# Where the routing's one-hot rows are issued between the operations of an attention tile

## The chip, the cores and the metric

One core of a Trainium2 chip. The metric is the device time of one execution in microseconds (us); lower is better. The engines of the core are named as in the profile: PE (TensorE, matrix products and transposes; PEld is its weight load), DVE (VectorE), ACT (ScalarE), POOL (GpSimd) and SP (SyncE, which here only issues DMAs). Each engine runs its own list of instructions in the order in which the kernel's text emits them; between engines, semaphores hold an instruction until its operands are there and its destination is free.

## The reference

Attention over pooled keys and values for 8 batches, 8 heads, 576 positions and a head width of 64, and then a mixture of experts with one expert for each token:

```python
k_p = k.reshape(B, H, Sp, 8, D).mean(axis=3)
v_p = v.reshape(B, H, Sp, 8, D).mean(axis=3)
scores = scale * np.matmul(q, k_p.transpose(0, 1, 3, 2))
scores = scores - np.max(scores, axis=-1, keepdims=True)
attn = np.exp(scores)
attn = attn / (np.sum(attn, axis=-1, keepdims=True) + 1e-09)
x = np.matmul(attn, v_p)                          # to 4608 tokens of 512
...
logits = x @ w_gate + modality_bias[modality_id]  # 8 experts
e_idx = np.argmax(logits, axis=1)
gate_w = softmax(logits)[np.arange(N), e_idx]
for e in range(E):
    mask = e_idx == e
    h = np.maximum(x[mask] @ w1[e], 0.0)
    out[mask] = gate_w[mask, None] * (h @ w2[e])
```

## The kernel before

**Attention.** The 4608 tokens are 36 tiles of 128. A step handles two tiles (one, in the steps that join the last 64 positions of two batches); there are 20 steps, five for each pair of batches, and a 21st pass that drains the last. The loop is software-pipelined: pass n makes the scores of its own second half and of the first half of step n + 1, and turns the probabilities of step n - 1 into output. For each half, PE writes the scores to PSUM (`s_pe`, L533), DVE takes the maximum of each row (`s_dve`, L540) and subtracts it (L543), and ACT takes the exponential (`s_act`, L555 and L556). For each tile of the step before, PE transposes the probabilities (L562, L574), ACT copies them (L567, L581), PE multiplies them with the values and with the gate's weights (`a_pe`, L597 and L601), and DVE divides (`x_dve`): the sum (L620), its reciprocal (L622), the gate's logits (L624), and the output's halves (L626, L631; for tiles of groups 2 and 3 ACT copies the second half undivided, L629). The result of `a_pe` has a single buffer in PSUM, so the products of a tile can begin when the tile before has been divided. POOL meanwhile pools keys and values by folding them in half three times (`fold`, L304 to L306).

**Routing.** The 36 tiles make four groups of nine. When a group's logits are there, `route` computes, by some 20 small DVE operations, the chosen expert (L680 to L691), the gate (L708 to L713, with the DMAs that write it beside the tokens) and the rank of each token within its expert. The counting is a set of matmuls (`pe` in `route`, L698 to L702), and what follows it (L725 to L736) splits the rank into a low part of 7 bits and a high part. Last come nine one-hot rows (L738), one for each tile: 128 x 128 in bf16, one where the column equals the token's low part. The rows are the left operand of a later product that turns ranks into lists of token numbers.

For group 0, `first_expert` (L748 to L754) follows: it finds the expert of the first token and loads it into a register of SP, so that the weights of that expert can be fetched early. For group 1, `early_table` follows: a count (`count`, a matmul on PE, L783), DVE operations (L793 to L799), the product of the rows with token numbers (`product`, L789), DVE operations that finish the indices (L763 to L767), and four gathers (L143, indirect DMAs that POOL issues) that fetch the tokens of the first two slots of 256 into `xg`. In step 17 PE transposes the first slot's gathered tokens (`x_transposes`, L161; ACT and DVE split them into two parts, L163 and L164), and from step 18 on the first matmuls of the experts (`first0`) run between the last attention steps.

**The order.** It is written out by hand. The DVE work of groups 0 to 2 stands in a list, `drip`, to which passes 6, 11 and 16 append a group's operations. Places in the loop called `gap` take up to n operations off its head: two between maximum and subtraction, one behind the sum, one behind the reciprocal, two at the end of a tile's division, and two more in the loop behind each place where a tile is divided. Functions in `held` (the matmuls of `route`, `count` and `product`) are not taken by a `gap`. They leave through `release`, at one place in each pass, just behind the scores' matmuls of the second half:

```python
            if due:
                release()
...
            run(hook_2, n)
            finish()
            due = bool(drip) and drip[0] in held
            if two:
                a_pe(old[1])
            if two:
                x_dve(old[1])
```

So `due` is set in one pass, ahead of the second tile's division, and acts in the next. Other work is bound to fixed passes by hooks: the transposes of the gathered tokens to passes N - 3 = 17 (`hook_2` and `hook_3`), and splits of the experts' weights to `hook_1` to `hook_3` (ACT L829, DVE L139).

**The experts.** Behind the attention, 18 or more slots of 256 tokens go through their expert's two matrices (PE L170 and L1155), with weights loaded by SP (L126, L129), split by ACT (L136) and DVE (L139), gathered by POOL (L143) and scattered to the output (L1141). The last group's routing is issued by hand in the first of these slots.

Of the kernel before, what the change touches and what calls it, by code (L numbers as in the profile page):

```python
# [30 lines left out]
def kernel(  # L31
# [31 lines left out]
    GROUPS = [(GT * i, GT) for i in range(B // 2)]  # L63
# [50 lines left out]
    def load_regs(s, e_ap, c_ap):  # L114
        e = nc.values_load(e_ap, engines=SP_ENGINE, min_val=0, max_val=E - 1,
                           skip_runtime_bounds_check_because="a sum over at most one expert's index")
        c = None
        if c_ap is not None:
            c = nc.values_load(c_ap, engines=SP_ENGINE, min_val=0, max_val=1,
                               skip_runtime_bounds_check_because="a comparison's result")  # L120
        regs[s] = (e, c)
# [69 lines left out]
    with ExitStack() as actx:  # L191
# [281 lines left out]
                tile_group[t] = (g, t - t0)  # L473
        drip, held, stores = [], set(), []

        def gap(n=2):

            for _ in range(n):
                if drip and drip[0] not in held:
                    drip.pop(0)()  # L480

        def release():
# [120 lines left out]
        def x_dve(t):  # L603
            n, z = tile_step[t]
            g, gi = tile_group[t]
# [24 lines left out]
            else:  # L630
                nc.vector.tensor_tensor(xo[:, 0:D // 2].rearrange("p (h d) -> p h d", h=4),  # L631
                                        avv[:, 0, :, 0:HD], rb[:, 0].to_broadcast([P, 4, HD]), op=ALU.mult)
            gap(2)

            if mixed:
                for y in range(2):
# [25 lines left out]
        def route(g):  # L662

            t0, n = GROUPS[g]
# [13 lines left out]
            ops = []  # L678
# [57 lines left out]
            add(lambda: V.tensor_copy(rh[:, sl], rki))  # L736
            for i in range(n):
                add(lambda i=i: V.tensor_scalar(arow[:, t0 + i, :], iota_b, rkf[:, i:i + 1], None, op0=ALU.is_equal))  # L738
            return ops

        def first_expert():

            V = nc.vector
            t8 = ap.tile([P, E], F32, name="t8")
            e0 = ap.tile([P, 1], F32, name="e0")
            rot = ap.tile([P, E], F32, name="rot")
            return [
                lambda: V.tensor_mul(t8, e0oh, iota_f[:, 0:E]),  # L748
                lambda: V.reduce_sum(e0, t8, axis=AX.X),
                lambda: (V.tensor_copy(meta0, e0[0:1, :]), load_regs(0, meta0[0:1, 0:1], None)),  # L750
                lambda: V.tensor_scalar(rot, iota_f[:, 0:E], e0, None, op0=ALU.subtract),
                lambda: V.tensor_scalar(t8, rot, 0.0, float(E), op0=ALU.is_lt, op1=ALU.mult),
                lambda: V.tensor_add(rot, rot, t8),
                lambda: V.tensor_tensor(lmat, rot.rearrange("p (o e) -> p o e", o=1).to_broadcast([P, E, E]),  # L754
                                        rot.rearrange("p (e o) -> p e o", o=1).to_broadcast([P, E, E]), op=ALU.is_lt),
            ]
# [53 lines left out]
        def at(hook, n, *fns):  # L810
            hook.setdefault(n, []).extend(fns)

        for n, (b, jj, _) in enumerate(steps):
            if b + 1 < B:
                if jj == 0:
                    m = n if b else n + 1
# [3 lines left out]
                if jj == 1:  # L820
                    m = n if b else n + 1
# [9 lines left out]
        for g in range(len(GROUPS) - 1):  # L831
            n = s1_of[2 * g + 1] + 2
            def start(g=g):
                ops = route(g)
                drip.extend(ops)
                if g == 0:
                    drip.extend(first_expert())
            at(hook_0, n, start)
            if g == EARLY_GROUPS - 1:
                at(hook_0, n, lambda: drip.extend(early_table()))  # L840
# [66 lines left out]
        for n in range(N + 1):  # L907
# [39 lines left out]
            run(hook_q, n)  # L947
            if old:
                x_dve(old[0])
            gap(2)  # L950
            if nxt and n:
                q_act(n + 1, 1)
            if has:
# [18 lines left out]
                x_dve(old[1])  # L972
            if n == 0:
                v_gate(0)
            gap(2)
            if n != N - 1:
                run(hook_3, n)
            finish()
        while drip:
            release()  # L980
            gap()
        loads(N + 1)
        last_route = route(len(GROUPS) - 1)
        for fn in last_route[:7]:
# [337 lines left out]
```

## Time and profile before

| | us |
|---|---|
| median of 3 runs | 634.19 (633.3 to 634.3) |
| the profiled execution | 631.66 |
| its span, first to last instruction | 629.9 |
| all one-hot rows of the attention passes, first to last start | 84.7 to 172.6 |
| first gather of the early slots, start | 144.7 |
| last attention matmuls and first slot, about | 185 |

All times of instructions count from the start of the span. In a timeline a line has the start, the time from the first instruction's start to the last one's end, the engine, the line of the kernel, the operation, output and inputs with their shapes, and how many instructions it merges; in brackets stands how long the engine had been idle before it and what ended the wait. In the chain of waits a line has the start, the share of the chain's time, and what ran. A group line of the source view has shortest, median and longest duration in ns.

### The profile page before, as it was taken

What the parts mean: (1) busy time and instruction counts of PE and PEld (TensorE: products, weight loads), DVE (VectorE), ACT (ScalarE), POOL (GpSimd) and SP (SyncE); (2) the same over time, 40 slices, a digit from 0 to 9 for tenths busy, and PEclk for the clock granted to TensorE, in tenths of its full rate; (3) what the DMA queues carried; (4) which work ended last, traced back from release to release, by engine and by line L of the source; (5) the groups of instructions that cost most, each with busy time, mean ns of one, the idle gap of its engine ahead of it and who ended that gap; (6) DMA issues with size and microseconds to landing.
All of it is one profiled execution on the core that took longest, in us unless ns stands there. A gap on an engine that the chain in (4) does not pass through costs nothing.

```text
span 629.9 us, 12488 instructions
## 1 busy us (share of the span) xinstructions
PE 601.1 (95%) x4223; PEld 544.8 (86%) x4223; DVE 409.1 (65%) x802; ACT 347.6 (55%) x666; POOL 237.8 (38%) x326
## 2 busy tenths in 40 slices
PE   4799999999999999999999999999999999999992
PEld 3699888897898898999999999999999999999991
DVE  4767888778957487656656566566566656656641
ACT  2667677887532555555555555555555555555540
POOL 5789968742000341331332331331331241331331
PEclk9899999999999999999999999999999999999997
DMA  9999969864113620120220460120135310120120
GB/s 252 308 284 350 355 199 362 261 209 137 53 70 110 227 69 17 52 69 7 64 69 16 153 223 31 50 68 18 53 91 183 132 56 18 53 69 18 52 70 19
DMA packets 63481, 77.12 MB, mean 122 GB/s; under 512 B 15535, under 2 KB 42159, under 8 KB 63408
## 3 DMA queue, kind: packets, MB, share of 16 engines
q1 hardware_dynamic: 57168, 55.98, 28.2%
q0 software_dynamic: 6240, 20.26, 10.0%
q8 instruction: 35, 0.57, 0.4%
q14 instruction: 38, 0.31, 0.2%
HBM read 119.94 MB, written 19.71 MB: 222 GB/s over the span
## 4 chain that ended last, share of the span: by engine, by line
PE 78%; DMA 6%; DVE 5%; issue 4%; ACT 3%; SPq 1%; POOL 1%; POOLq 0%; ACTq 0%; DVEq 0%
PE op L1155 29%; PE hp L170 29%; PE av L597 5%; PE sc L533 4%; PE av L601 2%; PE xt L161 2%; PE pq L508 2%; DMA out_dram<-ob,sidx 2%; PE pp L562 1%; PE ph L170 1%; DMA xg<-xs,gidx 1%; DMA k<-in_k_dram 1%; DMA raw<-in_moe_w_dram 1%; DVE kp L309 1%; DVE sb L543 1%
## 5 line engine op out<-in xcount | busy, mean ns | idle before, releaser
L136 ACT CAST hl<-raw 128x1024 fp32r<-128x1024 f32 x138 | 144.8, 1049 | 138.7 <-PE op L1155 134.7
L170 PE MATMUL hp<-xh,hl 128*128 128x256 f32 x1152 | 186.1, 284 | 0.0
L170 PEld LDWEIGHTS hp<-xh,hl 128*128 128x128 f32 x1152 | 166.1, 189 | 10.5
L139 DVE TENSOR_TENSOR hl<-raw,hl 128x1024 fp32r<-128x1024 f32 x144 | 175.0, 1217 | 0.0
L1155 PE MATMUL op<-hl,hh 128*128 128x512 f32 x554 | 173.5, 394 | 0.0
L1141 POOL DMA_INDIRECT out_dram<-ob,sidx x36 | 52.5, 1457 | 289.6 <-DVE ob L1137 184.5
L174 DVE SCALAR_TENSOR_TENSOR hlo<-hp,hh 128x256 fp32r<-128x256 f32 x139 | 58.7, 423 | 136.4 <-ACT hh L172 123.8
L1155 PE MATMUL op<-hl,hlo 128*128 128x512 f32 x277 | 108.4, 391 | 0.0
L1155 PEld LDWEIGHTS op<-hl,hh 128*128 128x128 f32 x554 | 94.8, 189 | 12.1
L170 PE MATMUL hp<-xl,hl 128*128 128x256 f32 x576 | 92.0, 282 | 0.0
L172 ACT ACTIVATE hh<-hp 128x256 fp32r<-128x256 f32 x139 | 53.3, 383 | 49.7 <-PE hp L170 47.8
L170 PEld LDWEIGHTS hp<-xl,hl 128*128 128x128 f32 x576 | 79.0, 190 | 0.0
L1155 PEld LDWEIGHTS op<-hl,hlo 128*128 128x128 f32 x277 | 52.0, 188 | 11.7
L597 PE MATMUL av<-vw,pt 128*128 128x146 f32 (+1 forms) x320 | 50.4, 297 | 1.4 <-ACT pt L567 0.9
L143 POOL DMA_INDIRECT xg<-xs,gidx x40 | 44.2, 1105 | 16.5 <-issue 10.4
L152 POOL TENSOR_TENSOR xg<-xg 128x256 f32<-128x256 f32 x34 | 31.2, 918 | 34.9 <-DMA xg<-xs,gidx 34.9
L597 PEld LDWEIGHTS av<-vw,pt 128*128 128x128 f32 (+1 forms) x320 | 40.3, 182 | 3.8 <-ACT pt L567 2.3
L533 PE MATMUL sc<-kt,qt 128*128 128x144 f32 x256 | 38.0, 292 | 0.0
L164 DVE TENSOR_TENSOR xl<-xt,xh 128x512 fp32r<-128x512 f32 x38 | 24.6, 685 | 17.1 <-ACT xh L163 17.1
L533 PEld LDWEIGHTS sc<-kt,qt 128*128 128x128 f32 x256 | 34.2, 195 | 0.2
L540 DVE TENSOR_REDUCE mx<-sc 128x8 f32<-128x576 f32 (+1 forms) x40 | 27.7, 692 | 10.0 <-PE sc L533 8.3
L601 PE MATMUL av<-vw,pt 128*128 128x146 f32 (+1 forms) x160 | 30.7, 295 | 0.4
(236 smaller groups left out, 713.0 us busy)
## 6 DMA issues: line engine op xcount, KB each, us to landing
raw<-in_moe_w_dram SPq DMA_DIRECT2D x304, 256.0 KB
xs<-xb SPq DMA_DIRECT2D x16, 528.0 KB
k<-in_k_dram SPq DMA_DIRECT2D x7, 1024.0 KB
v<-in_v_dram SPq DMA_DIRECT2D x7, 1024.0 KB
q<-in_q_dram SPq DMA_DIRECT2D x6, 1024.0 KB
q<-in_q_dram SPq DMA_DIRECT2D x4, 512.0 KB
v<-in_v_dram SPq DMA_DIRECT2D x16, 128.0 KB
xs<-xb SPq DMA_DIRECT2D x8, 132.0 KB
```

Of the source, the lines that this page charges most:

```text
L136: nc.scalar.copy(hl[f][:, 0, :], raw[f])
L139: eng.tensor_sub(hl[f][:, 1, :], raw[f], hl[f][:, 0, :].bitcast(F32))
L143: nc.gpsimd.indirect_dma_start(out=xgs[(2 * s + tt) % len(xgs)], out_offset=None, in_=xs[0:rows, :], in_offset=IndirectOffsetOnAxis(idx[:, ...
L152: nc.gpsimd.tensor_tensor(xv, xv, x[:, RX:RX + H // 2].rearrange("p (h o) -> p h o", o=1).to_broadcast([P, H // 2, HD]), op=ALU.mult)
L170: nc.tensor.matmul(ph, hl[f][:, w, d * P:(d + 1) * P], x[:, d, :], start=(n == 0 and d == 0), stop=(n == 2 and d == ND - 1))
L172: nc.scalar.activation(hh, ph, AF.Relu)
L174: nc.vector.scalar_tensor_tensor(hlo, ph, 0.0, hh.bitcast(F32), op0=ALU.max, op1=ALU.subtract)
L533: nc.tensor.matmul(dst, qt[:, i, :], kt[b % NB][:, :, h * SPL:(h + 1) * SPL], start=True, stop=True)
L597: nc.tensor.matmul(av[hs, u, 2 * VC * gg:2 * VC * (gg + 1)], pt[:, c, hs], vw[y][:, c].rearrange("p a x -> p (a x)"), start=(gg == 0), sto ...
L601: nc.tensor.matmul(dst4[hs], pt4[:, hs], v4[y][:, 2 * u:2 * u + 2, :], start=False, stop=True)
L1141: nc.gpsimd.indirect_dma_start(out=out[:, :], out_offset=IndirectOffsetOnAxis(idx.bitcast(U32), 0), in_=ob, in_offset=None, bounds_check=N ...
L1155: nc.tensor.matmul(o[tt], l[:, ts_], hl[f][:, w, D:2 * D], start=(f == 0 and n == 0), stop=(f == NF - 1 and n == 2))
```

## The change

The rows of a group are put in a set, `rows`. A `gap` takes a row off the head of the list only when it is called with `any_`, which three places do: the end of a tile's division, the two places in the loop behind it, and the loop that empties the list. Between maximum and subtraction, behind the sum and behind the reciprocal, a row at the head of the list is left there, and what stands behind it too. For group 0, `first_expert` now comes ahead of the nine rows; for the others the order within the list is as it was. The operations themselves, their number and the passes that append them are the same.

```diff
-        def gap(n=2):
+        rows = set()
+
+        def gap(n=2, any_=False):
             for _ in range(n):
-                if drip and drip[0] not in held:
+                if drip and drip[0] not in held and (any_ or drip[0] not in rows):
                     drip.pop(0)()
...
-            gap(2)
+            gap(2, True)
 
             if mixed:
...
                 add(lambda i=i: V.tensor_scalar(arow[:, t0 + i, :], iota_b, rkf[:, i:i + 1], None, op0=ALU.is_equal))
+            rows.update(ops[-n:])
             return ops
...
                 ops = route(g)
-                drip.extend(ops)
+                m = GROUPS[g][1]
+                drip.extend(ops[:-m])
                 if g == 0:
                     drip.extend(first_expert())
+                drip.extend(ops[-m:])
...
             if old:
                 x_dve(old[0])
-            gap(2)
+            gap(2, True)
...
             if n == 0:
                 v_gate(0)
-            gap(2)
+            gap(2, True)
...
         while drip:
             release()
-            gap()
+            gap(2, True)
```

## The prediction

> **What bounds the kernel now.** I read the page first, for the engines' shares, and then the chain of work that ended last, for the stretch in which one-hot rows are made.
>
> ```profile
> span 629.9 us, 12488 instructions
> PE 601.1 (95%) x4223; PEld 544.8 (86%) x4223; DVE 409.1 (65%) x802; ACT 347.6 (55%) x666; POOL 237.8 (38%) x326
> ...
> L738 DVE TENSOR_SCALAR arow<-iota_b,rkf x36: 194/242/898, 84.7 to 198.2; 128x128 bf16<-128x128 bf16 x36
> ...
> 84.79 0.54 DVE arow L738 x2
> ...
> 124.43 0.53 ACT pe L555
> ```
>
> TensorE (PE) is busy 95% of the span, so a microsecond of DVE work counts only where PE, directly or through ACT, waits for it, and a stall put on PE is lost for good unless PE would have idled there anyway. The third line is the rows' own group (source line view): 36 instructions, 194 ns at best, 898 at worst. The last 9 are issued in the expert phase and stay. So 27 move: nine for each of the routing groups 0, 1 and 2. The chain has two of them at 84.79, between a maximum (L540) and its subtraction (L543); around 124 us, where group 1's rows lie, it runs through ACT instead.
>
> **Part 1: what the pairs and reciprocals get back.** Timelines of DVE, POOL and ACT:
>
> ```profile
> 75.79 0.76 DVE L540 TENSOR_REDUCE mx<-sc 128x8 f32<-128x576 f32 x1
> 76.66 0.76 DVE L543 TENSOR_TENSOR sb<-sc,mx 128x576 f32<-128x576 f32 x1
> ...
> 84.04 0.74 DVE L540 TENSOR_REDUCE mx<-sc 128x8 f32<-128x576 f32 x1
> 84.71 0.45 DVE L738 TENSOR_SCALAR arow<-iota_b,rkf 128x128 bf16<-128x128 bf16 x1
> 85.24 0.74 DVE L543 TENSOR_TENSOR sb<-sc,mx 128x576 f32<-128x576 f32 x1
> ...
> 84.38 0.73 POOL L304 TENSOR_TENSOR k<-k 128x256 f32<-128x256 f32 x1
> ...
> 68.52 0.50 DVE L689 SCALAR_TENSOR_TENSOR lgr<-lgr,w 128x72 f32<-128x72 f32 x1
> ...
> 68.48 0.46 POOL L305 TENSOR_TENSOR k<-k 128x128 f32<-128x128 f32 x1
> ...
> 86.02 0.63 ACT L555 ACTIVATE pe<-sb 128x512 f32<-128x512 f32 x1 [0.73 <-DVE sb L543]
> ```
>
> A bare pair takes 0.87 us from start to start (75.79 to 76.66); with two rows in it 1.20 (84.04 to 85.24). The first row ends at 85.16, 0.05 after the POOL fold that began at 84.38 (ends 85.11): it was held until that fold was over. Of the 0.33 us at most that this pair could return, nothing comes: group 0's rows now stand behind the seven operations of first_expert, so L748 and L749 take their place in this very pair. L748 multiplies two tensors in SBUF, and such an operation is held too: L689 at 68.52 ends at 69.02, 0.08 after the fold begun at 68.48. I take 0; the bounds are a gain of 0.33 (ACT, waiting 0.73 here, starts earlier) and a loss of 0.1. The pairs of step 14 do become shorter, but there the chain lies on ACT (124.43 above), so again 0.
>
> **Part 2: four rows ahead of step 10.** By the hand-written order, step 9 now issues rows 0 to 3 behind its first tile and 4 to 7 behind its second; row 8 follows in step 10. The first four replace as many operations in that place and run beside an idle POOL. The other four stand ahead of step 10's maximum.
>
> ```profile
> 74.38 0.17 DVE L620 TENSOR_SCALAR r<-av 128x8 f32<-128x8 f32 x1 [0.99 <-PE av L601]
> ...
> 75.29 0.41 DVE L631 TENSOR_TENSOR xb<-av,r 128x256 f32<-128x256 f32 x1
> ...
> 88.36 0.74 DVE L543 TENSOR_TENSOR sb<-sc,mx 128x576 f32<-128x576 f32 x1
> 89.02 0.15 DVE L620 TENSOR_SCALAR r<-av 128x8 f32<-128x8 f32 x1
> ...
> 89.95 0.41 DVE L631 TENSOR_TENSOR xb<-av,r 128x256 f32<-128x256 f32 x1
> ...
> 93.29 0.17 DVE L620 TENSOR_SCALAR r<-av 128x8 f32<-128x8 f32 x1 [0.65 <-PE av L601]
> 94.71 0.76 DVE L540 TENSOR_REDUCE mx<-sc 128x8 f32<-128x576 f32 x1
> ...
> 94.63 0.45 POOL L306 TENSOR_TENSOR vp<-v 128x128 f32<-128x128 f32 x1
> 95.04 1.27 POOL L304 TENSOR_TENSOR v<-v 128x512 f32<-128x512 f32 x1
> 96.39 0.73 POOL L305 TENSOR_TENSOR v<-v 128x256 f32<-128x256 f32 x1
> ...
> 72.05 0.41 DVE L631 TENSOR_TENSOR xb<-av,r 128x256 f32<-128x256 f32 x1
> ...
> 72.61 0.74 PE L597 MATMUL av<-vw,pt 128*128 128x146 f32 x4 [0.42 <-DVE xb L631]
> ...
> 98.55 0.66 PE L597 MATMUL av<-vw,pt 128*128 128x146 f32 x4
> ...
> 196.87 1.54 DVE L738 TENSOR_SCALAR arow<-iota_b,rkf 128x128 bf16<-128x128 bf16 x9
> ```
>
> From L620 to L631 a bare tile takes 0.91 (74.38 to 75.29), one with two rows beside its reciprocal 0.93 (89.02 to 89.95): taking rows away from there is worth nothing, since it waits for L620's result anyway. So the second tile's L631 starts at 93.29 + 0.91 = 94.20 and ends at 94.61, where row 4 begins. Undisturbed rows take 1.54/9 = 0.17 each. POOL is in folds: I let rows 4 and 5 end with the fold begun at 94.63 (95.1) and rows 6 and 7 with the one begun at 95.04 (96.31), a held row and a free one to each: in the pair at 84.71 the second was through soon after the first, since the subtraction starts at 85.24. DVE is then free at 96.4 instead of 94.7. Then 0.87 to the subtraction, 0.66 to L620 (88.36 to 89.02), 0.91 to L631, 0.41 for it: 99.25. PE's next av matmuls use the one av buffer that L631 reads. Where DVE was late before, PE began 0.15 after L631's end (72.46 to 72.61): 99.4, against 98.55. **Term: +0.85 us.** If all four slip through, DVE is free at 95.3 (94.61 + 4 x 0.17) and the cost is 0; if one more fold (96.39, to 97.12) stands in the way, 1.65.
>
> **Part 3: the early gather, one step later.** A matrix product waiting in the queue is marked held, and is released one step on only if it heads the queue when `due` is set, just before the second tile's division. For group 1, step 14 used to have all rows out by then. Now rows 7 and 8 still head the queue; `due` stays false, and count goes out in step 16 instead of 15, the product in 17 instead of 16, the gather of the first slots' tokens likewise. But the transposes that read it stay in step 17.
>
> ```profile
> 144.25 0.16 DVE L765 TENSOR_SCALAR gidx<-t0ix 128x4 int32<-128x4 f32 x1
> ...
> 144.71 1.25 POOL L143 DMA_INDIRECT xg<-xs,gidx  x1 [4.60 <-DVE t0lo L766]
> ...
> 149.68 0.22 DVE L691 TENSOR_TENSOR oh<-w,m 128x72 bf16<-128x72 f32 x1
> ...
> 150.34 2.35 DVE L139 TENSOR_TENSOR hl<-raw,hl 128x1024 fp32r<-128x1024 f32 x2
> 152.61 0.45 DVE L540 TENSOR_REDUCE mx<-sc 128x4 f32<-128x288 f32 x1
> ...
> 153.49 0.15 DVE L620 TENSOR_SCALAR r<-av 128x8 f32<-128x8 f32 x1
> ...
> 155.46 0.66 PE L161 MATMUL xt<-ident,xg 128*128 128x128 f32 x4 [1.01 <-ACT qt L514]
> ...
> DMA to landing us min/median/max: 3.3/3.7/5.3
> ...
> 159.57 0.20 PE L698 MATMUL sc<-oh,tri 128*128 128x72 bf16 x1
> ...
> 159.85 0.28 PE L574 MATMUL sc<-ident,pe 128*64 128x128 f32 x1
> 160.43 0.72 PE L597 MATMUL av<-vw,pt 128*64 128x146 f32 x8 [0.30 <-ACT pt L567]
> ...
> 171.69 0.17 DVE L620 TENSOR_SCALAR r<-av 128x8 f32<-128x8 f32 x1 [0.65 <-PE av L601]
> ```
>
> Group 2's routing slides a step too, so the 0.66 us of it ahead of L139 (149.68 to 150.34) goes: L139 starts about 0.7 earlier, and L540 of step 17 at 151.9. From it to L620 I take 1.0 (0.88 before, with two other fillers), and L765 0.08 later: 153.0. L765 to the gather is 0.46 (144.25 to 144.71): 153.45. With the median landing of 3.7 us the data are there at 157.15, while PE was at its transposes (L161) at 155.46. **Term: +1.69 us**, between 1.3 (landing 3.3) and 3.3 (5.3). POOL is otherwise idle there.
>
> The Trainium skill (DMA: Bandwidth & Descriptors, section Anatomy of one DMA — SWDGE (gpsimd) path) gives 2.0 us plus the bytes over 436e3 per us; for 128 rows of 2112 bytes that is an estimate of 2.62 us. By that rule the term would be 0.6; no gather of this trace lands before 3.3, so the row decides.
>
> Two small terms follow. The 0.66 us of routing now runs in step 17 ahead of the two L139 there, which eats what ACT and PE could catch up (0.30 of idle at 160.43): **+0.1**, between -0.3 and +0.4. Group 2's ten counting matmuls, 159.57 to 159.85, stood before an idle PE; in step 19 they stand in a stretch in which PE has no wait up to 171.69: **+0.28**. Group 2's nine rows then run in steps 19 and 20, behind divisions, where DVE idles before each next operation: 0, at most 0.3. SP's queue sees group 2's gate writes a step later and the expert's register load earlier; nothing that is near its time stands behind either: 0.
>
> **Sum**: 0 + 0.85 + 1.69 + 0.1 + 0.28 = +2.9 us on the path. The profiled execution took 631.66 us (span 629.9 and 1.76 around it), which is 2.53 under the median of the runs, 634.19. I add the sum to the median: **637.1 us**; a profiled execution of the changed kernel would take about 634.6.
>
> **Rivals.** (a) The forecast: both stalls, roughly as priced. 0.65. (b) Only the gather stalls, the rows of step 9 slipping between folds, or only the rows cost: +2.1 or, if the gather's wait is mostly taken back later, +1.2; 635.3 to 636.3. For it speaks that at 85.16 a second row passed at once; against it that PE shows no idle to take anything back between 163 and 171. 0.17. (c) The dear end: 1.65 for the rows, a gather that lands after 5.3 us as the only early one with a record did (+3.3), the small terms +0.4: 639.5. 0.08. (d) Not slower: the pairs are what counts. Its one mechanism is the subtraction at 85.24, for which ACT waits 0.73; its price is the 0.33 of that pair, perhaps 0.5 with ACT's next waits; it decides only if the gather lands within 2.0 us of its issue (153.45 to 155.46), or the order of release is not as I read it, so that no term of part 3 applies, and the folds let the rows pass. 633.7. The 0.73 speaks for it, the 3.3 us minimum against it. 0.10. That the change does nothing can't be: each engine runs its own list in the order written.
>
> **How the numbers follow.** A measurement of this kernel can tell about 0.2%, or 1.3 us, from no change. (a) and (c) are slower by more; (b) is mostly so (0.13 of its 0.17); of (d) 0.03 is faster by more. So slower 0.86, same 0.11, faster 0.03. The range takes in (b) and (c) up to what the bounds make: 634.9 (rows free, shortest landing, 0.3 taken back, and the runs' own half microsecond) to 639.3.
>
> **What would show it.** Step 17's transposes (L161) should be waiting for a DMA of the gather by 1.5 to 2.5 us, with POOL's first gather at about 153 to 155 instead of 144.7; L783 a step later than now. At about 99 us PE's av matmuls should wait for DVE's L631, with rows of 0.4 to 1.2 us before step 10's maximum. After 190 us everything should be shifted by one constant. I am wrong if PE's transposes don't wait; if the shift at 120 us is negative, the pairs mattered more than I allow.

## The result and the profile after

| | us | ratio to before, 95% interval |
|---|---|---|
| before, median | 634.19 | |
| changed, median of 5 runs | 641.72 (638.2 to 643.41) | 1.012 [1.0088, 1.0152] |
| forecast | 637.1 (634.9 to 639.3) | |
| changed, the profiled execution | 638.2, span 636.5 | |

The change costs 7.5 us. The direction is as forecast, the size is not. All lines of the kernel behind the edited place are 3 higher in the changed kernel (L540 is L543, L738 is L741), and those in the expert phase 6 higher (L1155 is L1161).

The page of the changed kernel, its first lines:

```profile
span 636.5 us, 12491 instructions
...
PE 601.1 (94%) x4223; PEld 544.0 (85%) x4223; DVE 412.0 (65%) x802; ACT 347.8 (55%) x666; POOL 233.2 (37%) x326
```

PE is busy for 601.1 us, exactly as before. The 6.6 us by which the span grew are waits of PE and nothing else; 1.2 of them lie ahead of the first moved row. The rows' own line in the source view (shortest, median, longest of one, in ns):

```profile
L741 DVE TENSOR_SCALAR arow<-iota_b,rkf x36: 235/245/1310, 91.3 to 203.7; 128x128 bf16<-128x128 bf16 x36
```

The longest row took 1310 ns instead of 898, and the last one starts later than before. Now the three places that the prediction named. DVE's timeline of the changed kernel (start, time to the last one's end, both in us):

```profile
95.41 0.41 DVE L634 TENSOR_TENSOR xb<-av,r 128x256 f32<-128x256 f32 x1
95.74 2.57 DVE L741 TENSOR_SCALAR arow<-iota_b,rkf 128x128 bf16<-128x128 bf16 x4
98.23 0.74 DVE L543 TENSOR_REDUCE mx<-sc 128x8 f32<-128x576 f32 x1
...
111.52 0.92 DVE L724 TENSOR_TENSOR cum<-cum,dc 128x8 bf16<-128x8 bf16 x1
```

POOL's timeline of it:

```profile
95.77 0.45 POOL L306 TENSOR_TENSOR vp<-v 128x128 f32<-128x128 f32 x1
96.19 1.27 POOL L304 TENSOR_TENSOR v<-v 128x512 f32<-128x512 f32 x1
97.53 0.73 POOL L305 TENSOR_TENSOR v<-v 128x256 f32<-128x256 f32 x1
...
111.15 1.27 POOL L304 TENSOR_TENSOR v<-v 128x512 f32<-128x512 f32 x1
...
156.78 1.25 POOL L143 DMA_INDIRECT xg<-xs,gidx  x1 [5.37 <-DVE t0lo L770]
```

PE's timeline of it:

```profile
101.12 0.77 PE L600 MATMUL av<-vw,pt 128*128 128x146 f32 x4 [1.24 <-DVE xb L634]
...
160.57 0.63 PE L161 MATMUL xt<-ident,xg 128*128 128x128 f32 x4 [2.79 <-ACT hl L833]
```

**Rows ahead of step 10's maximum.** Four rows that need 0.7 us undisturbed took 2.57 us. They end at 98.31, 0.05 us behind the third of the three folds (97.53 + 0.73 = 98.26), and only then comes the maximum. PE's av matmuls, which had no wait there before, wait 1.24 us for DVE's L634. **A second hold in step 12**: L724 took 0.92 us and ends at 112.44, 0.02 behind the fold begun at 111.15. In the trace of before the same operation took 0.12:

```profile
108.89 0.12 DVE L721 TENSOR_TENSOR cum<-cum,dc 128x8 bf16<-128x8 bf16 x1
```

**The gather.** POOL's first one starts at 156.78 instead of 144.71, and PE idles 2.79 us ahead of the transposes of step 17, against 1.01. The bracket names ACT, which had been done; in the second profile of this kernel (`again`, below) the same wait of 2.73 us is put down to the gather's DMA.

**Behind 190 us**, where one constant shift was forecast, the shift stays constant to 570 us, and then grows by another 1.1 us in this profile and by 2.3 in `again`. That second profile took 642.01, near the median, and is the better one to read. The slot that I call the last full one, here and in the expectations, has its first division at 577.58 us in the kernel before; two more slots end behind it. POOL's scatters of that slot and its next gather, first in the kernel before, then in `again`:

```profile
578.61 1.78 POOL L1141 DMA_INDIRECT out_dram<-ob,sidx  x1 [12.29 <-DVE ob L1137]
583.07 1.42 POOL L1141 DMA_INDIRECT out_dram<-ob,sidx  x1 [2.68 <-PE op L1155]
584.79 1.04 POOL L143 DMA_INDIRECT xg<-xs,gidx  x1 [0.30 <-PE hp L170]
```

```profile
587.00 1.78 POOL L1147 DMA_INDIRECT out_dram<-ob,sidx  x1 [12.66 <-DVE ob L1143]
593.60 1.78 POOL L1147 DMA_INDIRECT out_dram<-ob,sidx  x1 [4.82 <-ACT hh L172]
595.68 1.04 POOL L143 DMA_INDIRECT xg<-xs,gidx  x1 [0.30 <-issue]
```

A slot has two scatters and then the gathers for the next slot. The second scatter writes the same tensor as the first, and its issue is held until the first has landed (3.6 us behind its issue before, 5.8 in `again`, by the DMA line of the view of tile ob). So it starts 2.68 or 4.82 us behind the end of the first, the gathers behind it are later by as much, and PE finds its rows missing:

```profile
600.63 0.66 PE L161 MATMUL xt<-ident,xg 128*128 128x128 f32 x4 [1.15 <-POOL xg L152]
601.96 0.66 PE L161 MATMUL xt<-ident,xg 128*128 128x128 f32 x4 [0.67 <-POOL xg L152]
```

I call this the **late end** below. In the profile of before there is no such wait at this place.

**The clock.** PE's windows of `again` (stretch, its length, PE busy, count, granted clock, DMA), and behind them those of the changed kernel's first profile:

```profile
162.00:164.00 2.00, 1.81 (x12) 0.81 0.68 188
164.00:166.00 2.00, 2.00 (x10) 0.50 0.59 186
166.00:168.00 2.00, 2.00 (x16) 0.83 0.22 93
168.00:170.00 2.00, 1.98 (x26) 1.00 0.43 177
```

```profile
160.00:162.00 2.00, 1.43 (x12) 1.00 0.79 203
162.00:164.00 2.00, 2.00 (x19) 1.00 0.60 201
```

In `again` the granted clock falls to half behind the 2.73 us wait and is back at 1.00 from 168 us on; the same wait without that fall is in the first profile.

### The profile page after: what moved, and what is told of

Its sections match the earlier page's. It is cut to its first block, busy times and chain, and to the rows that moved or that the text cites. A ratio compares the mean times of both kernels' runs of the same rounds, so it can differ in the third digit from the quotient of the medians.

```text
span 636.5 us, 12491 instructions
## 1 busy us (share of the span) xinstructions
PE 601.1 (94%) x4223; PEld 544.0 (85%) x4223; DVE 412.0 (65%) x802; ACT 347.8 (55%) x666; POOL 233.2 (37%) x326
## 4 chain that ended last, share of the span: by engine, by line
PE 73%; DMA 9%; DVE 5%; POOL 4%; issue 4%; ACT 2%; SPq 1%; POOLq 0%; ACTq 0%; DVEq 0%
PE op L1161 29%; PE hp L170 29%; DMA k<-in_k_dram 4%; PE av L600 4%; PE xt L161 2%; DMA out_dram<-ob,sidx 2%; PE av L604 2%; PE sc L536 2%; PE ph L170 1%; PE pq L511 1%; DMA xg<-xs,gidx 1%; POOL v L304 1%; DMA raw<-in_moe_w_dram 1%; PE pp L565 1%; POOL v L305 1%
## 5 line engine op out<-in xcount | busy, mean ns | idle before, releaser
L1161 PE MATMUL op<-hl,hh 128*128 128x512 f32 x554 | 173.5, 394 | 0.0
L1161 PE MATMUL op<-hl,hlo 128*128 128x512 f32 x277 | 108.5, 392 | 0.0
L1161 PEld LDWEIGHTS op<-hl,hh 128*128 128x128 f32 x554 | 94.8, 189 | 12.1
L1161 PEld LDWEIGHTS op<-hl,hlo 128*128 128x128 f32 x277 | 52.0, 188 | 11.8
L152 POOL TENSOR_TENSOR xg<-xg 128x256 f32<-128x256 f32 x34 | 27.8, 818 | 36.5 <-DMA xg<-xs,gidx 36.4
L543 DVE TENSOR_REDUCE mx<-sc 128x8 f32<-128x576 f32 (+1 forms) x40 | 27.7, 693 | 10.0 <-PE sc L536 8.7
```

Source lines behind the costliest of these rows:

```text
L152: nc.gpsimd.tensor_tensor(xv, xv, x[:, RX:RX + H // 2].rearrange("p (h o) -> p h o", o=1).to_broadcast([P, H // 2, HD]), op=ALU.mult)
L1161: nc.tensor.matmul(o[tt], l[:, ts_], hl[f][:, w, D:2 * D], start=(f == 0 and n == 0), stop=(f == NF - 1 and n == 2))
```

## The experiments

Each kernel was timed in five rounds beside the kernel before on the same chip. The medians of the kernel before differ by up to 0.8 between these sessions. In the table "rows" is PE's wait ahead of L161 in step 17 (in `kept_busy` ahead of its fillers), "scatter" POOL's wait ahead of the second scatter of the last full slot, and "division" DVE's wait ahead of that slot's first division (L1137), all in us from the profiled execution.

| run | median | before | ratio, 95% interval | rows | scatter | division |
|---|---|---|---|---|---|---|
| again | 642.16 | 633.99 | 1.0135 [1.0117, 1.0153] | 2.73 | 4.82 | 1.10 |
| g0_only | 635.83 | 633.99 | 1.0026 [1.0007, 1.0044] | 1.01 | 2.80 | 0.74 |
| g1_only | 638.85 | 633.99 | 1.0079 [1.0062, 1.0095] | 2.75 | 4.57 | 1.10 |
| due_ahead | 635.91 | 633.99 | 1.003 [1.0011, 1.0048] | 1.01 | 2.57 | 0.73 |
| late_gather | 638.43 | 634.21 | 1.0071 [1.0041, 1.0101] | 2.73 | 4.00 | 1.10 |
| kept_busy | 640.7 | 634.21 | 1.0118 [1.0088, 1.0147] | 2.71 | 2.55 | 1.10 |
| later_transposes | 638.39 | 634.21 | 1.0069 [1.0039, 1.0099] | 1.11 | 4.55 | 1.10 |
| groups_1_and_2 | 635.27 | 634.21 | 1.0018 [0.9995, 1.0042] | 1.01 | 2.55 | 0.73 |
| rows_after_step_10s_first | 633.98 | 633.77 | 1.0004 [0.9988, 1.002] | 1.01 | 2.75 | 0.73 |
| gather_behind_L397 | 633.96 | 633.77 | 1.0004 [0.999, 1.0017] | 1.02 | 2.76 | 0.74 |
| gathers_first_before | 633.89 | 633.77 | 0.9999 [0.9986, 1.0013] | 1.02 | 0.30 | 0.73 |
| gathers_first_after | 638.27 | 633.77 | 1.0066 [1.0049, 1.0082] | 2.72 | 0.63 | 1.10 |
| kept_busy_2 | 641.63 | 633.39 | 1.0111 [1.0078, 1.0145] | 0.73 | 4.53 | 1.11 |
| late_gather_alone | 636.24 | 633.39 | 1.0036 [1.0014, 1.0058] | 2.49 | 2.75 | 0.74 |
| group_2_late | 636.25 | 633.39 | 1.0042 [1.0024, 1.0061] | 0.44 | 4.83 | 1.11 |
| causes_removed | 633.45 | 633.39 | 1.0006 [0.9985, 1.0026] | 1.01 | 2.66 | 0.74 |
| stores_as_before | 640.04 | 634.15 | 1.0077 [1.0056, 1.0098] | 2.76 | 4.97 | 1.11 |
| gates_behind_store | 633.33 | 634.15 | 0.9993 [0.9975, 1.0012] | 1.01 | 2.73 | 0.73 |

### The change again, and group by group

`again` is the changed kernel as it is.

> The changed kernel as it is, once more beside its parts. My theory now: two stalls on PE that the profile of the changed kernel shows (about 2.1 us in steps 9 to 12, about 2.1 us in steps 17 to 19) make +4.3 us; what is beyond that in the first comparison (+7.5 in the medians) came from differences between executions that lie ahead of the first moved row (+1.2 at 80 us) or in the expert phase (+1.1 at the end). Expected by it: +4 to +5 us over before. Rival: the change itself makes the early phase or the tail slower; then +7 again, with the shift at 80 us again above 1 us.

It came to 8.2 above the kernel before, not 4 to 5. Of the rival's two places, the tail is slower by the change; the early phase isn't, as the account below shows.

`g0_only`:

```diff
-            rows.update(ops[-n:])
+            if g == 0:
+                rows.update(ops[-n:])
```

> Rows of group 0 alone are kept out of the pairs and reciprocals, with first_expert ahead of them; groups 1 and 2 as before. Theory: the four rows ahead of step 10's maximum, held by POOL's folds, delay DVE by 2.3 us and PE by 1.5 to 2.1 us: +1.5 to +2.1, with the first gather and step 17's transposes on time. Rival (the pairs matter): between -0.5 and 0.

`g1_only` has `if g == 1:` there, and the list's old order:

```diff
-                drip.extend(ops[:-m])
+                drip.extend(ops)
                 if g == 0:
                     drip.extend(first_expert())
-                drip.extend(ops[-m:])
```

> Rows of group 1 alone are kept out of the pairs and reciprocals; groups 0 and 2 in the old order. Theory: count, product and gather one step later, step 17's transposes wait for the gather: +2.1 (1.7 at the transposes, 0.4 behind them). Rival: if group 0's rows are the whole cost, 0.

Group 0's rows cost 1.8 us, group 1's 4.9. `g0_only` has no wait for the gather, and `g1_only` no wait at step 10, so the two mechanisms of the prediction belong to the groups that it named. But 4.9 us is far more than the 2.1 of the gather, and the sum of the two is 6.7, where `again` has 8.2 (a difference that the intervals don't separate).

### The product let go in time

`due_ahead` is the changed kernel; `due` is also set when up to four rows stand ahead of a held product and two tiles are left to take them.

```diff
-            due = bool(drip) and drip[0] in held
+            ahead_rows = 0
+            while ahead_rows < len(drip) and drip[ahead_rows] in rows:
+                ahead_rows += 1
+            due = ahead_rows < len(drip) and drip[ahead_rows] in held and (
+                ahead_rows == 0 or (two and ahead_rows <= 4))
```

> The changed kernel, except that due is also set when at most four rows stand ahead of a held matmul, so that rows 7 and 8 of group 1 no longer keep count back for a step; every row is still issued behind a division only. Theory: the gather is back in step 16 and its 2.1 us go, the rest stays: 2.1 less than the changed kernel, +1.5 to +2.5 over before. Rival (the delay of the gather is hidden and something else costs): no difference from the changed kernel.

POOL's and PE's timelines of it:

```profile
149.46 1.25 POOL L143 DMA_INDIRECT xg<-xs,gidx  x1 [4.60 <-DVE t0lo L770]
```

```profile
160.22 0.66 PE L161 MATMUL xt<-ident,xg 128*128 128x128 f32 x4 [1.01 <-ACT qt L517]
```

The gather is back in step 16, PE's wait is 1.01 as before, and 6.3 us of the 8.2 are gone (642.16 to 635.91), the late end among them. So all of that hangs on the list being one step late, not on where rows stand.

`groups_1_and_2` is the same without group 0 (`if g:` ahead of `rows.update`, the list in its old order).

> Rows of groups 1 and 2 moved as in the change, the product let go in time as in the run with the early release, and group 0 left as it was before. Theory: only group 0's four rows ahead of step 10's maximum were left in that run (1.9 us), so this one is level with before: 634.0, between 633.3 and 634.7. Rival: moving group 1's or group 2's rows costs or gains something of its own: 635 or more, or 633 or less.

635.27, half a microsecond outside what was expected and among the rival's times, but with an interval that holds 1: whether these two groups cost anything by themselves isn't settled by the times. In the profiles of the three kernels that let the product go early (`due_ahead`, `groups_1_and_2`, `causes_removed`) the divisions fall behind by another 0.4 us between 131.58 and 148.73 of before.

### The lateness without the rows

`late_gather` is the kernel before, with rows in their old places, and the product held back one step:

```diff
-            due = bool(drip) and drip[0] in held
+            due = bool(drip) and drip[0] in held and n != 15
```

> The kernel before, rows where they were, with one thing changed: the waiting product (and so the table, the gather and group 2's routing) is let go one step later. If lateness of the gather is the whole of part 3: PE's transposes (L161) wait 2.7 to 2.8 us in step 17 as in the changed kernel, +2.1 us behind it. If the late end is a consequence of the late gather as well, the second scatter of the last slots waits 4.0 to 4.8 instead of 2.7 us and the whole is +4 us (638). If the late end has to do with the rows' places instead, the whole is +2 (636). If the order of the rows mattered beside the gather's lateness, step 17 shows less than +2.

Both came. Divisions are shifted by 2.7 us up to 148.73 of before (the early phase of this execution) and by 4.8 from 171.69 on, which is 2.1 for step 17. The second scatter waits 4.00, and the rows' places have no part in either. But of the 2.8 us that this profile loses behind 190 us, only 0.9 lie in the last slots: 1.9 are two waits of PE for gathered tokens, at 480 and 505 us, and `gather_behind_L397`, which has no late end, has one such wait as well.

### Where the four rows stand

`rows_after_step_10s_first` is `g0_only` with no row let go behind the second tile of step 9:

```diff
-            gap(2, True)
+            gap(2, tile_step[t] != (8, 1))
...
                 v_gate(0)
-            gap(2, True)
+            gap(2, n != 9)
```

> Group 0's rows alone are moved (groups 1 and 2 as before), and no rows are let go behind the second tile of step 9: rows 4 to 7 stand behind the first tile of step 10, ahead of the maximum there, and row 8 behind its second. POOL is in its folds there as well. Theory: what group 0 costs (1.8 us with rows 4 to 7 ahead of step 10's maximum) is the place ahead of a maximum in a step whose division PE waits for; every such place beside the folds costs it, so 635.0 to 636. Rival: only step 9's place is bad, since PE has slack later in step 10: 634.0 to 634.5.

The rival was right. DVE's timeline of this kernel, step 10:

```profile
101.80 1.16 DVE L741 TENSOR_SCALAR arow<-iota_b,rkf 128x128 bf16<-128x128 bf16 x4
102.88 0.74 DVE L543 TENSOR_REDUCE mx<-sc 128x8 f32<-128x576 f32 x1
```

Four rows ahead of another maximum, one division later, again beside POOL's folds: held more briefly (1.16 instead of 2.57), and nothing is lost (633.98 against 633.77). It is the one place ahead of step 10's first maximum that costs.

### The transposes later

`later_transposes` is the changed kernel:

```diff
-        at(hook_2, N - 3, lambda: x_transposes(0, xg, (0,)))
-        at(hook_3, N - 3, lambda: x_transposes(0, xg, (1,)))
+        at(hook_3, N - 3, lambda: x_transposes(0, xg, (0,)))
+        at(hook_1, N - 2, lambda: x_transposes(0, xg, (1,)))
```

> The changed kernel with the two groups of transposes of the gathered rows moved half a step back on PE: the first behind step 17's second tile, the second into step 18, both still ahead of the first product that reads them. Theory: the wait for the gather is what part 3 and the clock cost; with 2.6 us more until PE needs the data, the wait is 0 to 0.3, and 2.1 (wait) + 0.9 (clock) come back: 639.2; 637 if the late end goes as well. Rival: the lateness is only handed on to the first product of the expert phase, which waits for the split of the transposed rows instead: 641.5 to 642.2.

```profile
161.16 0.63 PE L161 MATMUL xt<-ident,xg 128*128 128x128 f32 x4 [1.11 <-ACT hl L833]
```

In PE's timeline the wait is 1.11, and the shift across step 17 only 0.34 (3.89 to 4.23): the wait for the gather is hidden. The median gains 3.8 on `again`, and still stands 4.2 above before. So neither that wait nor a clock that falls behind it makes the late end, which this profile shows in full.

### The clock

`kept_busy` has twelve idle transposes on PE ahead of those that wait:

```diff
+        def keep_busy():
+            for _ in range(12):
+                nc.tensor.transpose(corner(P), ident, ident)
+        at(hook_2, N - 3, keep_busy)
         at(hook_2, N - 3, lambda: x_transposes(0, xg, (0,)))
```

> The changed kernel with twelve 128x128 transposes of the identity on PE, into a corner of PSUM that nobody reads, ahead of the transposes that wait for the gather: 1.8 us of the 2.7 us wait are filled with work of no use. Theory: the granted clock falls after the bare wait in most executions, and costs 0.9 us; filled, it stays at 1.00 and every run shows a clock above 0.988, time 641.0 to 641.5 against 642.2 for the changed kernel. Rival: the clock has nothing to do with the wait; then the clocks stay between 0.984 and 0.990 and the time 642.2, or more if the dummies delay the transposes.

```profile
161.62 1.53 PE L856 MATMUL sc<-ident 128*128 128x128 f32 x12 [2.71 <-DVE sb L546]
162.99 0.60 PE L161 MATMUL xt<-ident,xg 128*128 128x128 f32 x4
```

The fillers didn't fill the wait. They write into a score tile and so wait themselves for the subtraction that reads it; they ran behind the idle time, not in it, and the run says nothing of what a filled wait does. `kept_busy_2` puts them into the transposes' own buffer:

```diff
             pt = ps_tr.tile([P, ND, P], F32, tag="tr", name=f"xt_{s}_{tt}")
+            if (s, tt) == (0, 0):
+                for d in range(12):
+                    nc.tensor.transpose(pt[:, d % ND, :], ident, ident)
```

> The changed kernel with twelve transposes of the identity into the very buffer that the waiting transposes write afterwards, so that they run in the 2.7 us wait and not behind it. Theory: PE's idle shrinks to about 1 us in front and the granted clock stays at 1.00 in the profile and above 0.990 in every run; the shift across step 17 is 2.1 us as in the profile without the fall, and the time 640.5 to 641.3 against 642. Rival: the clock still falls in some executions, with a lower clock than 0.99 in two or more runs, and the time stays at 642.

```profile
159.81 1.53 PE L162 MATMUL xt<-ident 128*128 128x128 f32 x12 [0.45 <-ACT qt L520]
162.07 0.66 PE L164 MATMUL xt<-ident,xg 128*128 128x128 f32 x4 [0.73 <-DMA xg<-xs,gidx]
```

Now PE idles 0.45 and 0.73, its clock stays at 1.00, the shift across step 17 is 2.10, and all six runs show a mean clock of 0.990 to 0.993 (`again`: 0.987 to 0.991). The time is 641.63 all the same (637.37 to 643.11). The fall of the clock is real where it occurs; six runs that spread so far can't tell its 0.9 us from nothing, but they show that most of the 8 us is there without it.

### The late end

`gathers_first_after` and `gathers_first_before` are the changed kernel and the kernel before, with the next slot's gathers ahead of the second scatter in POOL's list:

```diff
-        def evac(tts=(0, 1)):
-            for tt in tts:
+        def evac(between=lambda: None):
+            for tt in (0, 1):
...
+                if tt:
+                    between()
                 idx = (sidx0 if s < EARLY_SLOTS else sidx)[:, 2 * s + tt:2 * s + tt + 1]
...
-                    tail()
                     if nxt and s >= EARLY_SLOTS:
-                        gather(s + 1, gidx, 2 * (s + 1), xg)
+                        tail(lambda: gather(s + 1, gidx, 2 * (s + 1), xg))
+                    else:
+                        tail()
```

> The changed kernel with the same edit. Theory: the late end (2.3 us in one profile of it) comes from the last slots' gathers standing behind a second scatter that waits for the landing of the first; ahead of it they start at 2.8 us instead of 8.1 to 9.7 us behind the division, the transposes never wait, and the time is 639.8 to 640.4 instead of 642.2. Rival: the gathers land late for another reason (the weights' loads); then transposes still wait and the time stays at 642.

> The kernel before with the two gathers for the next slot put ahead of the second scatter in POOL's list, in every slot of the expert phase: they no longer wait for the landing of the first scatter. Theory: in the kernel before the gathers are early enough at nearly every slot (one wait of PE of 0.7 us in the profile), so 633.3 to 634.2. Rival: the second scatter, now later, holds buffers or shares the DMA engines with the gathers: 635 or more.

POOL and PE of `gathers_first_after`:

```profile
586.10 1.76 POOL L1149 DMA_INDIRECT out_dram<-ob,sidx  x1 [15.47 <-PE hp L170]
588.17 1.16 POOL L143 DMA_INDIRECT xg<-xs,gidx  x1 [0.30 <-issue]
589.64 1.99 POOL L143 DMA_INDIRECT xg<-xs,gidx  x1 [0.31 <-issue]
592.26 1.01 POOL L1149 DMA_INDIRECT out_dram<-ob,sidx  x1 [0.63 <-DMA out_dram<-ob,sidx]
```

```profile
598.42 1.03 PE L161 MATMUL xt<-ident,xg 128*128 128x128 f32 x8
```

The gather starts 0.30 us behind the first scatter, and all eight transposes run together with no wait. The changed kernel comes to 638.27, 3.9 below `again` (3.7 when each is taken against the kernel before beside it), more than the 1.8 to 2.4 expected; the kernel before gains nothing (633.89 against 633.77). So the gathers that stand behind a slowly landing scatter are the largest part of what the forecast missed, and only the changed kernel loses by them.

What in the early part brings this about? Five runs looked for it. (Where an expectation speaks of 24.21 or 24.58 us, it means the distance of the last full slot's first division from that of the slot before; the 0.37 between them is the difference in the table's last column.) `gather_behind_L397` gives POOL's list the order that it has with a late gather, with the gather still in time:

```diff
-            ops += [lambda: [gather(s, gidx0, 2 * s, xg, T_EARLY * P) for s in range(EARLY_SLOTS)]]
+            ops += [lambda: at(hook_2, 16, lambda: [
+                gather(s, gidx0, 2 * s, xg, T_EARLY * P) for s in range(EARLY_SLOTS)])]
```

> The kernel before with its early gathers behind the last scaling (L397) in POOL's list, as they stand in the kernels with the late gather, but still in step 16: they start at about 148 instead of 144.7 and land before the transposes ask for them at 155.5. Theory: the late end goes with the lateness of the gather or what it moves in the other queues, so nothing of it is seen: 634.2, the last scatter pair 4.3 to 4.6 us apart, last slot's division 24.21 us after the one before. Rival: POOL's order alone makes the late end: 24.58 and 636 to 637.

Level with before: POOL's order is not it. `late_gather_alone` issues product, table and gather in step 17, with group 2's routing ahead of them; `group_2_late` does the reverse, with group 2's routing started two steps later (in the changed kernel its matmuls come one step later):

```diff
-            ops += [product]
-            ops += finish_table(lambda: psm["t"], C, gidx0, sidx0, "t0")
-            ops += [lambda: [gather(s, gidx0, 2 * s, xg, T_EARLY * P) for s in range(EARLY_SLOTS)]]
+            rest = []
+            rest += finish_table(lambda: psm["t"], C, gidx0, sidx0, "t0")
+            rest += [lambda: [gather(s, gidx0, 2 * s, xg, T_EARLY * P) for s in range(EARLY_SLOTS)]]
+            at(hook_1, N - 3, product, lambda: drip.__setitem__(slice(0, 0), rest))
```

```diff
-            n = s1_of[2 * g + 1] + 2
+            n = s1_of[2 * g + 1] + 2 + 2 * (g == 2)
```

> The kernel before with the product, the table and the gather issued in step 17, and group 2's routing ahead of them, earlier than before, not later. Transposes wait 2.7 us or a little more (+2.1). If the lateness of the gather makes the late end: the division of the last full slot comes 24.58 us after the one before, the second scatter waits 4 to 4.8 us, +1 to +2 more: 637.5 to 638.5. If group 2's routing and its place in SP's list make it: 24.21 and 636.3.

> The kernel before with group 2's routing started two steps later, so that SP's list is that of the late kernels, and the gather in time. If the lateness of the gather makes the late end, nothing is seen of it: 24.21 and 634.0 to 634.6. If group 2's routing makes it: 24.58, and 635.5 to 636.5.

DVE's first division of the last full slot: before, `late_gather_alone`, `group_2_late`.

```profile
577.58 0.75 DVE L1137 TENSOR_SCALAR ob<-op,xg 128x512 f32<-128x512 f32 x1 [0.74 <-PE op L1155]
```

```profile
584.82 0.75 DVE L1138 TENSOR_SCALAR ob<-op,xg 128x512 f32<-128x512 f32 x1 [0.74 <-PE op L1156]
```

```profile
580.70 0.75 DVE L1137 TENSOR_SCALAR ob<-op,xg 128x512 f32<-128x512 f32 x1 [1.11 <-PE op L1155]
```

The gather alone, late, makes no late end (2.75 us ahead of the second scatter); group 2's routing alone, late, with the gather in time, makes it (4.83) and costs 2.9 us. The same holds for all twenty profiles of this study: the ten of kernels in which group 2's routing is late have 1.10 or 1.11 ahead of that division, the ten others 0.73 or 0.74. The long wait of the second scatter goes with it, but not in every execution: `kept_busy` has 1.10 and a scatter wait of 2.55.

The one order behind the attention passes' end that I found group 2 to change by itself is SP's, where its gate writes fall behind a store. `stores_as_before` takes the changed kernel and puts that store off (`while stores and n != 18:`); `gates_behind_store` takes the kernel before and puts the gate writes behind the store:

```diff
                 V.reciprocal(gate[:, sl], sm)
+                if g == 2:
+                    at(hook_0, 18, store)
+                else:
+                    store()
+
+            def store():
                 for z in range(2):
```

> The changed kernel, with one store of a tile pair (step 18's) put off by a step, so that the gate writes of group 2 stand ahead of it in SP's list, as in the kernel before. If that order makes the late end: the last full slot's division comes 24.21 us after the one before, the second scatter waits 2.6 to 2.8 us, and the time is 638 to 639 instead of 642. If it only goes with it: 24.58 and 641 to 642.5.

> The kernel before, with the gate writes of group 2 put behind the store of the next tile pair in SP's list and nothing else moved. If that order makes the late end: 24.58, a second scatter that waits 4 us or more, and 635.5 to 636.5. If it only goes with it: 24.21 and 633.4 to 634.2.

Both say no: 1.11 and 4.97 stay in the one, 0.73 and 2.73 in the other. (640.04 lies between the two expectations, and below `again` by more than the intervals of the two; by its waits that run has the late end. What the store's place is worth by itself is open.)

The traces go further than these runs. That division doesn't wait for PE, though the bracket names it: the products that it reads end at 576.66 before and at 584.69 in `again`, 0.92 and 1.28 ahead of it. What DVE does there is to load two numbers into registers (`used` and `half`), which isn't counted as busy. The source view of these lines, in the kernel before and in `again`:

```profile
L1261 DVEq TENSOR_LOAD <-meta x1: 547/547/547, 576.4 to 576.4; - x1
L1263 DVEq TENSOR_LOAD <-meta x1: 320/320/320, 577.1 to 577.1; - x1
```

```profile
L1267 DVEq TENSOR_LOAD <-meta x1: 540/540/540, 584.5 to 584.5; - x1
L1269 DVEq TENSOR_LOAD <-meta x1: 318/318/318, 585.5 to 585.5; - x1
```

Between the end of the first load and the start of the second lie 0.1 us before and 0.5 in `again`. In nineteen of the twenty traces DVE pauses so, for 0.37 us more than the same pair of instructions takes in the others, and always ahead of the 960th instruction that the trace records on it. In the kernel before that is the first one behind the division, and the pause is hidden while the division runs. The changed kernel has three more semaphore instructions on DVE (1015 instructions for 1012), `group_2_late` has one more, and so the pause stands ahead of the division, and the scatter behind it is late by 0.37. (In the twentieth, `late_gather_alone`, which has one instruction fewer, no pause shows.)

The DMA records of the traces show why the scatter then lands late. Its 80 packets meet a load of instructions, 16 KB in one packet (queue q8 of the page). In the ten profiles without the late end this load starts when the scatter's last packet has ended, or up to 0.2 us later, and that packet ends 3.2 to 3.4 us behind the scatter's start. In eight of the ten others the load starts among the packets, the last three to five of them start only as it ends, and the last one ends after 4.5 to 5.5 us. In `gathers_first_after` the load starts among them too, but gathers run there as well. In `kept_busy` the load has ended ahead of the first packet, and the scatter is in time (3.2): that is the exception above. So the kernel before gets through by luck, with 0.2 us or less to spare. All this is read from traces; no run moved the pause or the load alone.

### The causes taken out

`causes_removed` is `due_ahead` with the two `gap` edits of `rows_after_step_10s_first`: all rows of the three groups still stand behind divisions alone.

> The change, rows of all three groups still behind divisions alone, with two things put right: the waiting product is let go in time (up to four rows ahead of it), and no rows behind the second tile of step 9, so that none stand ahead of step 10's maximum. Theory: these are all its causes of loss, so the time is that of the kernel before: 633.7 to 634.7. Rival: something else of the change costs: 635 or more; or the shorter pairs are worth something once the losses are gone: 633.3 or less.

633.45 against 633.39: level. The change's idea, done without its two side effects, neither costs nor gains. No kernel of the study beats the kernel before by more than the measurement can tell.

## Why the prediction was right in direction and wrong in size

**Part 1, nothing from the shorter pairs: right.** `causes_removed` has all of them and is level.

**Part 2, +0.85 for four rows: mechanism right, size low.** PE's av matmuls moved from 98.55 to 101.12, and the division ahead of the rows from 93.29 to 94.50, so the rows cost 2.57 - 1.21 = 1.36 there. The step that failed is "a held row and a free one to each": two folds were to let four rows through, and it took three, the case priced at 1.65 as the dear bound (it measured 1.36). Then 0.7 more in step 12, by L724, an eight-column addition: a later DVE met a fold that it had not met before (0.92 instead of 0.12). The prediction had no term for work that is shifted into a fold. Together 2.1, in six of the nine profiles with these rows. In the other three (`g0_only`, `kept_busy`, `stores_as_before`) the rows took 2.01 and L724 0.11 or 0.12, and the shift is 1.5; in the medians `g0_only` costs 1.8. The page SBUF — State Buffer of the Trainium skill (section SBUF: two separate sides) calls the port pair that DVE and GpSimd share an exclusive lock, held for a whole instruction. The trace agrees: rows and L724 end 0.05 and 0.02 us behind a fold.

**Part 3, +1.69 and the small terms, 2.07 in all: right.** 2.12 in the changed kernel's profile (divisions of before at 148.73 and 171.69 shifted by 3.35 and 5.47), 2.1 in `late_gather`. What it lacked is the clock: of eight profiled executions in which PE idled 2.49 to 2.79 us there, the granted clock fell to 0.50 behind the wait in four (`again`, `gathers_first_after`, `late_gather_alone`, `stores_as_before`); in the twelve with a shorter wait there it never did. In `again` that made 2.96 out of 2.12 (5.04 to 8.00). The page TensorE: Matmul & The Clock Gate (section Why this matters for your kernels) warns of idle gaps over about 3 us and (Part 1) of a free-running window of some 3.4 us. Here shorter gaps were enough, in every second case; the slow stretch does last 3.4 us (below).

**"After 190 us everything should be shifted by one constant": wrong, and the costliest step.** Group 2's slide by a step was priced at 0.38 (its two small terms), with nothing behind 190 us. `group_2_late`, which slides it by two, costs 2.9 in the medians; its profile (638.28, above its median of 636.25) has 0.67 up to 190 us, 0.9 at about 500 and 3.7 in the last slots. Taking the second scatter out of the gathers' way gave the changed kernel 3.9 back. What the prediction took as given is that a later routing moves all that follows alike; by the traces, three more instructions in DVE's list move a pause of 0.37 us ahead of a division, and the scatter behind it into a load of instructions.

So the profile of `again` adds up: 2.15 for rows and L724, 2.96 in step 17, 2.3 in the last slots, 7.4 in all; its span is 10.3 longer than that of before, of which 2.9 lie ahead of the first moved row, at the division at 93.29. That last part is no effect of the change: the profiled execution of before was a quick one (631.66, median 634.19), and the profiles of six kernels that are the kernel before up to there (such as `gather_behind_L397`) are 1.1 to 3.7 later at that division, too.

**Still open.** Why DVE pauses at that place of its list, and whether moving the pause or the load of instructions by itself would take the late end away: no run tried it. Lateness of the gather, POOL's order and SP's order were tried and don't make it.

## What to carry to other kernels

A filler list with held entries is a schedule of its own: an entry that may only leave at fewer places delays everything behind it by whole steps, so follow each later entry to its reader before pricing the moved one. Small operations on DVE beside POOL's folds cost up to the rest of the fold, not their own 0.1 to 0.2 us, and a shift of DVE alone can move others into a fold. Look behind the last place that an edit touches: here a third to a half of the loss lay 400 us later, in gathers queued behind a scatter that waits for another's landing. Three instructions more in one engine's list were enough for that, so a time that rests on a margin of 0.2 us is partly luck.

## What the hardware showed that was not expected

- An idle stretch of PE of 2.49 to 2.79 us was followed by half the granted clock in four of eight executions. By the windows of `again` it lasted 3.4 us: 0.19 x 2 / 0.5 = 0.76 of the first, all 2 of the second, 0.17 x 2 / 0.5 = 0.68 of the third. It cost 0.9 us there. The same sum gives 3.4 in the other three. Gaps of 1.11 us or less at that place were never followed by it.
- Four 0.17 us rows took 2.57 us beside three folds (2.01 in three of nine profiles), and an addition of 128x8 elements took 0.92 instead of 0.12 beside one.
- The last packet of one scatter, with the same 80 packets in all, ended 3.2 to 3.4 us behind its start in eleven profiles and 4.5 to 5.5 in eight. It was late where a 16 KB load of instructions started among its packets, and in time where the load started behind them or had ended ahead of them.
- DVE paused 0.37 us ahead of the 960th recorded instruction of its list in nineteen of twenty profiles, whatever that instruction was.
